# One core, an attention and FFN kernel: the engines' instruction lists searched anew past batch 0's k

## The chip, the cores and the metric

The kernel runs on one core of one Trainium2 chip. A core has TensorE (PE; its weight loads are shown as PEld), VectorE (DVE), ScalarE (ACT), GpSimd (POOL) and SyncE (SP), each with an instruction list of its own that it works through in order, and DMA queues. The metric is device time in microseconds (us); less is better.

## What is computed

Four batches of eight heads, 768 positions, 64 wide. A small 8 x 8 matrix per head is normalized five times over rows and columns, mixes the eight blocks of k and of v, and attention then stays inside each block of 96 positions. The result, 3072 tokens of 512, goes through a two-layer network.

```python
P = sort_net                                   # (4, 8, 8, 8), five times:
    P = exp(P - max); P = P / rowsum; P = P / colsum
k_sorted = einsum('bhij,bhjcd->bhicd', P, k_b) # the same for v
scores = (1 / 8) * q_b @ k_sorted^T            # inside each block of 96
attn = softmax(scores)
x = (attn @ v_sorted) as (3072, 512)
h = x @ w_in                                   # 512 -> 2048
g = max(h, 0) + alpha * min(h, 0)
out = g @ w_out                                # 2048 -> 512
```

## The kernel before

**The work.** There are 32 groups, one for each batch and block of 96 positions: groups 0 to 7 are batch 0. For each batch, k is prepared in six units: POOL spreads a unit into `KSz` (`conv_k`, L672), PE multiplies it by the mixing matrix (`prep_k`, a "k block", L685), ACT or DVE evicts it into `KT`. v is prepared in eight units: a copy into `VDz` (`conv_v`; for batch 0 into a part of `hT`, which is still free), a product on PE (`prep_v`, a "v block", L726), an eviction into `VS`. `VDz` has four slots and `KSz` three, so a copy waits until the product on its slot's old content is done. Batch 0 takes other forms of both (L656, L731).

**A group** (`attention`) takes scores on PE (s1, L772 for batch 0, L769 later), their maxima on DVE (`nm` or `nf`, L778), in batch 0 a second pass of scores with the maximum subtracted (s2, L793 and L784) and one exponential on ACT into `ET` (L816); in the later batches eight exponentials into `Esb` (L805), which a DMA transposition on SP's queue turns into `ET` (L810). Then PE multiplies by v (o, L825), DVE takes a reciprocal and scales (`rec`, `xq`, L833 and L836), and a transposition, on PE in batches 0 and 1 (tr, L851, copied into `xT`) and by DMA later (L844), gives the FFN's input. q of batches 1 to 3 is turned by six DMA transpositions each (`turn_q`, L465).

**The FFN.** FFN1 (`ffn1`, L875) takes chunks of groups: two chunks of two groups (192 columns), then seven of four (384 columns), each in 16 blocks of four matmuls into one of two PSUM banks of `psH` (the first chunk uses `psP` as a third); ACT takes the negative part (`t`, L885), DVE combines it into `hT` (L888). FFN2 (`ffn2`, L914) makes 24 tiles of 128 tokens, each in four parts of four matmuls, which are evicted to `outstg` and stored by SP. The last tile is made in two halves.

**The order.** Every operation is added to a graph with what it reads and writes. A table `SEQ` lists all 1226 operations by number, in one order from which each engine's list is read off; a letter behind a number gives the engine for those that may run on several (`p` POOL, `a` ACT, `d` DVE; none: the first that is allowed). `arrange` walks the table and computes a planned start for each. Semaphore waits follow from the graph. The table is data in the kernel: nothing is searched when it is built.

**Identity products.** `fill` and `idle` then look for gaps in the planned PE list and put matmuls with the identity there (`warm`, L1041), 512 columns each, into a PSUM bank that nobody reads. They compute nothing that is needed. In the trace there are 55 of them: 51 into `psYP`, three into `psH` and one into `psO`.

Of the kernel before, what the change touches and what calls it, by code (L numbers as in the profile page):

```python
# [7 lines left out]
AP = bass.AP  # L8
# [24 lines left out]
0 2 11 3 7 4 8 1 22 9 14 42 28 43 44 19 45 46 5 47 18 48 49 15 50 51 39 52 53 6 54 55 56 25 57 58 29 59 60 61  # L33
23 62 63 12 64 65 66 132 89 37 67 83 68 81 31 69 84 70 32 87 71 13 10 91 88 85 72 40 73 74 90 130 75 76 86 41
77 133 78 82 79 131 92 80 93 134 138 102 94d 103a 26 104 147 95 105a 100 148 98 96d 97 108 99a 38 101d 109d
158 159 118 106a 119d 107a 35 114 160 149 36 115d 116 16 120 117a 112a 146 150 111 110d 113d 161 30 17 122 27
135 123a 24 121a 128 144 124 129d 126 143 125a 151 127d 21 145 136 152 137 162 153 163 164 154 183 155 165
166a 34 156 184 20 157a 167 141 192 33 185 168 193 140 169 194 142 186 170 201 195 139 247 246 249 248 253 252
171 202 198 196 203 204 199 197 187 219 200 220 205 216 213 217 214 218 206 221 215 228 207 188 225 189 222
272 226 229 227 223 230 234 224 260 235 237 236 261 190 262 250 191a 238 269 208 309 270 231 251a 209 239 174  # L40
210 402 401 232 233 240 211 257 254 271 263 212d 255a 290 256 310d 278 264 258 291 273 346 259a 265 266 304
312d 292 279 267 280 303 241 268 293 284 242 281 243 301 282 337 347a 283 274 300 338 302a 244 299 287 245d
285 339 286 311 351d 294 340 313 295 305 296 275 314 288 315 289 319 276a 177 297 306d 316 320 321 307 317 378
298a 318 178 325 308a 379 322 341 323 348 342 182 380 326 324 354 349a 327 328 343 352 180 329 331 353d 381
344 350 345d 356 179 332 330 382 357a 334 383 333 372 335 181 359a 336 360 384 363 361 387 364 362 418 393 403
388a 385 365 366 419 369 358 367 373 370 368 420 374 386d 355d 428 371 394d 391 421 429 434 390d 444 431 392a
435 389 395 432 375 430 436 446 396d 452 445 376d 397 433 404 449 453 437 398a 454 464 447 458 465 399 459 455
474 176 400a 460 405 448 175 456 173 450 466 406 478 451d 422 457 475 476 482 172 423 467 504 424 461 483 494
484 505 462 425 407 477a 463 414 495 426a 480 485 572 573 408a 481d 438 409 486 548 412 439 496 487 508 506
277 440 491 479 417 534 410 411 509 413 416 535 415 507d 441 488 492 497 442d 524 493 489 510 490 515 511a 377  # L50
525 512 516 549 517 513 526 514 468 536 518 537d 521 469 470 519 527 560 520 538 471 561 539a 542 522 472d 571
543 523 498 540 562 550 499 570 500 541d 501 545 544 502a 563 574 546 554 575d 596 547 555 605 557 556 606a
611 503 578 558 576 551 559 579 427 612 580 581 552a 597 584 577 582 533 590 583 585 598 586 528 443 587 529
530 609 613 636 531 599 614 625 532d 608 591 610a 626 588 569 607 592 589 627 637 564 615 616 473 565 634 566
619 635a 628 567 617 638 568d 593 639a 618 620 640 622 641a 621 645 600 594a 676 643 601 658 623 595 677 642
661 659 624 644 678 662 602 663 660 670 679 703 671 603 704 664 604a 647 667 705 665d 648 629 666 691 630 631
692 713 672 668 706 669 712 738 685 739 715 673 686 693 714 687 674 740 675 632 716 633d 688 717 718 697 719d
752 689 741 767 698 690 680 751 749 699 700 553 649 750d 720 701 646 694 702 721 777 722 723 695a 768 753 696
726 780 754a 681 732 682 724 748 727 725 683 733 769 747 728 734 707 729 708 770 709 755 730 742 731 756 778
710 802 779a 812 757 758 782 776 759 761 760 781 735 762 783a 763 657 764 803 736a 813 651 784 814d 849 787  # L60
785 743 765 786 788 653 804 744 654 789 766 745 852 771 793 772 773 805 846 815 794 837 796 816a 795 811 774
790 797 656 798 817 799 853 818a 791d 819 800 838 650 825 820 847 801 839 826 821 655 822 848 806 850 840 807
831 808 652 851a 872 832 883 827 792 823 833 880 824 854 881a 886 834 855 828 856 835 836 884 860 910 885a
829d 857 861 873 882 711 866 858 862 874 887 867 859 911 908 863 909d 888 875 864 841 865 889 900 912 684 890
891 913a 842 901 894 892 746 868 893 902 869 843 844 876 870d 914 897 895 877 896 919 903 898 915d 916 878 934
917 920 879 935 980 918 936 809 981 899 928 775 925 929 904 830 930 926 921 927 960 737 931 961 922 932 937
905 962 906 942 933 982 907 945 923a 963 986 946 948 987 943 949 944 988 938 950 939 940 954 947 989 1006 955
957 1007 810 983 958 1008 959 951 956 971 952d 964 968 972 1009 984a 973 1017 969 965 845 1032 970 977 966 974
941 978 990 979 975 1018 985 976 997 1033 994 924 998 1019 999 995 967 996 1003 991 1000 1004 1020 1005 1001
1034 1002 1023 992 1014 993 1010 1046 1011 1015 1012 1024 1047 1035 1016 1058 1025 1026 871 1059 1029 1027  # L70
1013 1048 1028 1030 1060 1031 1040 1021d 1043 1078 1041 1061 1036 1044 1079 1037 1042 1022 1084 1045 1052 1085
953 1049 1053 1086 1054 1080 1038 1055 1050d 1066 1056 1087 1062 1067 1115 1063 1068 1104 1057 1072 1064 1069
1105 1065 1116 1070 1071 1106 1117 1075 1088 1118 1076 1107 1089 1073 1077 1081 1074 1039 1095 1090 1082a 1092
1096 1051 1136 1097 1093 1119a 1094 1101 1091 1108 1102 1098 1120 1103 1137 1099 1109 1100 1121 1083 1110 1112
1122 1111 1160 1123 1113 1114 1127 1124 1128 1138 1129 1125 1126 1133 1130 1134 1161 1135 1131 1132 1145 1142
1146 1162 1147 1143 1144 1139 1148 1163 1149 1140a 1150 1151 1141 1154 1152 1181 1153 1155 1156 1157 1166 1158
1202 1159 1167 1168 1182 1172 1169 1173 1208 1174 1170 1171 1178 1175 1179 1183 1180 1176 1177 1190 1187 1191
1184 1192 1188 1189 1196 1185a 1193 1186 1197 1209 1198 1194 1195 1210 1164d 1199 1165 1203 1200 1201 1204
1220 1211 1205 1212d 1221 1213 1206d 1222 1223 1207 1214 1224 1215 1216 1225 1217 1218 1219
# [41 lines left out]
class _Graph:  # L121
# [79 lines left out]
    def arrange(self, table):  # L201
        assert len(table) == len(self.ops)
# [5 lines left out]
        done = set()  # L208
        for x in table:
            op = self.ops[int(x.rstrip("pad"))]  # L210
            e = letters.get(x[-1], op.engs[0])
            assert e in op.engs and op.deps <= done
            done.add(op.idx)
            at = max(free[e], self.ready_at(op, e))
            op.eng, op.start, op.pos = e, at, len(self.order[e])
            free[e], op.end = self.span(op, e, at, free, loads)
            self.order[e].append(op)
        return max(op.end for op in self.ops)

    def fill(self, make, unit, first, spans):  # L220

        out, last = [], self.ops[first].end + 300
        for op in self.order["pe"]:
            for lo, hi in spans:
                begin = max(last, lo)
                n = int((op.start - begin) * 0.9 / unit)
                if op.start <= hi and n > 0:
                    x = _Op("pe", lambda e, n=n: make(e, n), n * unit, 0.0, None, len(self.ops))
                    x.start, x.end, x.banks = begin, begin + n * unit, set()
                    x.deps.add(first)  # L230
                    self.ops.append(x)
                    out.append(x)
            out.append(op)
            last = max(last, op.end)
        for pos, op in enumerate(out):
            op.pos = pos
        self.order["pe"] = out

    def idle(self, make, unit, banks, lo, hi, least):

        used = {k: sorted((op for op in self.ops if k in op.banks), key=lambda o: o.start) for k in banks}
        out, last = [], 0.0
        for op in self.order["pe"]:
            n = int((op.start - last) * 0.85 / unit)
# [841 lines left out]
```

## Time and profile before

| | |
|---|---|
| median of 3 runs | 241.96 us (241.48 to 242.43) |
| the profiled execution: own time, span | 242.12 us, 240.1 us |
| granted TensorE clock | 1.00 |
| PE busy by the page | 231.3 us |
| DVE, ACT, POOL busy by the page | 172.4, 153.9, 99.8 us |
| identity products into `psYP`, busy | 15.1 us (51) |
| HBM read, written | 27.28 MB, 6.29 MB |

The span is what the profile shows from the first instruction to the last; the execution's own time has about 2.0 us more around it. Matmuls are pipelined, so their busy times overlap, and start to start is what a block costs PE. In the chain of waits each piece lasts until the next begins. In a timeline row the columns are start, length, engine, line, operation, tiles, shapes and count, and in brackets the idle time before it with what ended that. L12 is line 12 of the kernel.

### The profile page before, as it was taken

The numbers are of one execution on the slowest core, as the hardware profiler recorded it, in microseconds if no ns is written. First come the engines' busy times: TensorE is split into PE (matmuls) and PEld (weight loads), VectorE is DVE, ScalarE is ACT, GpSimd is POOL, SyncE is SP. The second block draws the span as 40 slices with busy tenths as digits, with TensorE's granted clock in tenths as the row PEclk, the third lists the DMA queues.
The fourth block names the chain that finished last, engine by engine and source line by source line (L and its number), as shares of the span: only waits on it lengthen the run. The fifth ranks groups of instructions, "written<-read, shape, count | busy, mean of one in ns | idle before, by whom it ended". The sixth has DMA issues, their size and how long they took to land.

```text
span 240.1 us, 6229 instructions
## 1 busy us (share of the span) xinstructions
PE 231.3 (96%) x2519; PEld 142.3 (59%) x2519; DVE 172.4 (72%) x348; ACT 153.9 (64%) x422; POOL 99.8 (42%) x146
## 2 busy tenths in 40 slices
PE   7889998999999999999999999999999999999995
PEld 3446676688566656655666566555655555555554
DVE  4756887998989888777958677756777666645542
ACT  4576466678978788977667778567756655444510
POOL 7989707924689964518859841000000000000000
PEclk9999999999999999999999999999999999999999
DMA  5999999999967999999749974593745426101023
GB/s 101 205 211 217 155 220 197 176 180 166 161 118 141 144 128 163 161 180 164 153 101 69 114 137 79 111 183 64 141 121 112 123 49 177 39 0 44 0 91 131
DMA packets 71981, 31.36 MB, mean 131 GB/s; under 512 B 64512, under 2 KB 67344, under 8 KB 71952
## 3 DMA queue, kind: packets, MB, share of 16 engines
q0 software_dynamic: 23408, 13.63, 42.6%
q1 hardware_dynamic: 48544, 17.33, 35.2%
q8 instruction: 20, 0.33, 0.6%
q14 instruction: 9, 0.07, 0.1%
HBM read 27.28 MB, written 6.29 MB: 140 GB/s over the span
## 4 chain that ended last, share of the span: by engine, by line
PE 71%; POOL 11%; DMA 10%; DVE 5%; issue 1%; ACT 0%; POOLq 0%
PE psH L875 29%; PE psYP L914 27%; DMA KS<-in_k_dram 10%; POOL VDz L428 5%; PE psS L914 4%; PE psO L825 3%; PE psS L769 3%; PE psYP L726 2%; PE psYP L685 2%; DVE hT L888 1%; POOL KSz L672 1%; POOL w_in_bf L959 1%; POOL VDz L512 1%; DVE VDz L428 1%; PE psO L914 1%
## 5 line engine op out<-in xcount | busy, mean ns | idle before, releaser
L875 PE MATMUL psH<-xT,w_in_bf 128*128 128x384 bf16 (+1 forms) x556 | 98.4, 311 | 0.6 <-DVE hT L888 0.4
L888 DVE SCALAR_TENSOR_TENSOR hT<-t,omaT,psH 128x384 bf16<-128x384 f32 (+1 forms) x139 | 77.7, 571 | 29.2 <-ACT t L885 27.5
L885 ACT ACTIVATE t<-psH 128x384 f32<-128x384 f32 (+1 forms) x139 | 62.7, 461 | 50.5 <-PE psH L875 49.2
L914 PE MATMUL psYP<-w_out_bf,hT 128*128 128x512 bf16 x336 | 82.9, 379 | 0.0
L875 PEld LDWEIGHTS psH<-xT,w_in_bf 128*128 128x128 bf16 x556 | 49.0, 98 | 29.2 <-DVE hT L888 4.1
L914 PEld LDWEIGHTS psYP<-w_out_bf,hT 128*128 128x128 bf16 x336 | 31.1, 98 | 30.3 <-DVE outstg L428 0.6
L805 ACT ACTIVATE Esb<-psS,nf 96x96 bf16<-96x96 f32 x192 | 46.2, 344 | 2.0 <-DVE nf L778 1.8
L428 POOL COPY VDz<-VST 64x384 bf16<-64x384 bf16 x40 | 34.1, 853 | 15.6 <-PE psYP L726 12.8
L672 POOL COPY KSz<-KS 64x512 bf16<-64x512 bf16 x36 | 22.0, 612 | 18.8 <-PE psYP L685 8.8
L778 DVE TENSOR_REDUCE nf<-psS 96x8 f32<-96x768 f32 x24 | 22.8, 948 | 5.5 <-PE psS L769 5.1
L836 DVE TENSOR_TENSOR xq<-psO,rec 96x512 bf16<-96x512 f32 x31 | 21.2, 683 | 0.6
L457 POOL DMA_DIRECT2D QN<-in_q_dram x24 | 19.9, 837 | 0.3 <-POOL QN L517 0.3
L1041 PE MATMUL psYP<-identb 128*128 128x512 bf16 x51 | 15.1, 417 | 0.7 <-ACT identb L428 0.7
L825 PEld LDWEIGHTS psO<-VS,ET 112*128 112x128 bf16 x248 | 11.3, 98 | 4.7 <-DVE xT L428 0.7
L769 PEld LDWEIGHTS psS<-KT,QTz 128*96 128x96 bf16 x192 | 11.9, 125 | 2.5
L833 DVE RECIPROCAL rec<-psO 96x8 f32<-96x8 f32 x31 | 6.2, 200 | 9.8 <-PE psO L825 9.8
L825 PE MATMUL psO<-VS,ET 112*128 112x65 bf16 x248 | 12.7, 194 | 0.4 <-DVE xT L428 0.3
L769 PE MATMUL psS<-KT,QTz 128*96 128x96 bf16 x192 | 12.6, 209 | 0.0
L428 ACT ACTIVATE VS<-psYP 112x512 bf16<-112x512 f32 x15 | 10.3, 686 | 3.1 <-PE psYP L726 2.6
L428 ACT ACTIVATE KT<-psYP 128x512 bf16<-128x512 f32 x15 | 8.9, 596 | 3.8 <-PE psYP L685 2.5
L726 PEld LDWEIGHTS psYP<-BDV,VDz 128*128 128x128 bf16 x192 | 8.0, 98 | 3.6 <-POOL VDz L428 0.8
L726 PE MATMUL psYP<-BDV,VDz 128*128 128x64 bf16 x192 | 9.6, 193 | 0.5 <-POOL VDz L428 0.5
(142 smaller groups left out, 204.0 us busy)
## 6 DMA issues: line engine op xcount, KB each, us to landing
out_dram<-outstg SPq DMA_DIRECT2D x23, 256.0 KB, 2.6
KS<-in_k_dram POOLq DMA_DIRECT2D x3, 768.0 KB, 8.7
QN<-in_q_dram POOLq DMA_DIRECT2D x24, 96.0 KB, 3.8
w_in_bf<-in_moe_w_in_dram POOLq DMA_DIRECT2D x4, 512.0 KB, 11.9
w_out_bf<-in_moe_w_out_dram POOLq DMA_DIRECT2D x2, 1024.0 KB, 23.3
VST<-in_v_dram POOLq DMA_DIRECT2D x4, 384.0 KB, 18.3
hT<-in_q_dram POOLq DMA_DIRECT2D x1, 768.0 KB, 7.0
VST<-in_v_dram POOLq DMA_DIRECT2D x1, 768.0 KB, 10.9
```

Source lines behind the costliest of these rows:

```text
L428: return e.activation(o, i, ACTF.Copy) if e is nc.scalar else e.tensor_copy(o, i)
L672: G.add(POOL, lambda e, hp=hp: e.tensor_copy(AP(KSz, hp * 64 * 3072 + u % 3 * 1024 + hp * 64, [[3072, 64], [128, 8], [1, 64]]), AP(KS[n], ...
L726: inst = e.matmul(AP(t, off + dd * 64, [[row, 128], [1, 64]]), AP(VDz, (u % VSL * 8 + dd) * 128, [[VSL * 1024, 128], [1, 128]]), AP(BDV, b ...
L769: inst = e.matmul(o, AP(QTz[n], hp * 3072 + h4 * 768 + i * 96, [[6144, 128], [1, 96]]), AP(KT[n], (h4 * 8 + i) * bk, [[ld, 128], [64, 2], ...
L778: G.add(DVE, lambda e: e.tensor_reduce(AP(nx, 0, [[8, 96], [4, 2], [1, 4]]), AP(psX, 0, [[1024, 96], [512, 2], [96, 4], [1, 96]]), AxisLis ...
L805: inst = e.activation(AP(Esb[me], p * 128, [[1024, 96], [64, 2], [1, 48]]), AP(psX, (p // 4) * 512 + (p % 4) * 96, [[1024, 96], [48, 2], [ ...
L825: inst = e.matmul(AP(psZ, hp * 512 + h4 * 68, [[1024, 128], [1, 65]]), AP(ET[me] if far else ET[m], pos(h4, hp) * 96, [[800, nk], [1, 128] ...
L836: G.add(DVE, lambda e: e.tensor_tensor(out=AP(xq[me], 0, [[512, 96], [256, 2], [64, 4], [1, 64]]), in0=AP(psZ, 0, [[1024, 96], [512, 2], [ ...
L875: inst = e.matmul(AP(pt, poff, [[1024, 128], [1, n]]), AP(w_in_bf, kt * DFF + ft * 128, [[KT_TILES * DFF, 128], [1, 128]]), AP(xT, kt * XR ...
L885: G.add(ACT, lambda e: e.activation(AP(t1[tb], 0, [[384, 128], [1, n]]), AP(pt, poff, [[1024, 128], [1, n]]), ACTF.Relu, scale=-1.0), t_ac ...
L888: G.add(DVE, lambda e: e.scalar_tensor_tensor(out=AP(hT, ft * RING + tok % RING, [[FT_TILES * RING, 128], [1, n]]), in0=AP(t1[tb], 0, [[38 ...
L914: inst = e.matmul(AP(bank[0], bank[1], [[1024, 128], [1, n]]), AP(hT, ft * RING + tok % RING, [[FT_TILES * RING, 128], [1, 128]]), AP(w_ou ...
```

## The change

The table `SEQ` is another from the place on where batch 0's k has been prepared, for all five engines. Ahead of that place (about 16 us in the trace) the lists are the same, except that what `fill` put there now stands in the table as entries. An entry such as `i3G` is three identity products into the bank with the letter G; `filler` makes an operation of it that waits for those who read that bank, and `fill` and `idle` are gone. The new table has 49 identity products: 31 up to and just behind batch 0's last k block, as before, and 18 more, the last two ahead of s2 of group 2.

Three kinds of operation may now run on more engines: batch 0's q evictions on ACT or DVE, batch 0's eight v copies and the copy `KTpad` on POOL, ACT or DVE. In the table, `KTpad` goes from POOL to DVE; of batch 0's v copies ACT has units 5, 0, 3, 4 and 6 (before 0, 1 and 6), DVE 1 and 2 (before 3, 4 and 7) and POOL 7 (before 2 and 5). The q evictions stay on ACT. The DMA transpositions were taken as longer in the search that gave the table; no duration in the kernel's code is changed for that.

Part of PE's list, from o of group 0 to the first v block of batch 1 (`1.3` is block 3 of FFN1's chunk 1; `t0.1` part 1 of FFN2's tile 0; `k2` k block 2 of batch 1; `I` identity products):

```
before: o0 s1(2) tr1 tr0 spread 1.0 s2(2) 1.3 1.1 1.2 s1(3) o2 1.6 1.5 1.4 s2(3) 1.9 1.8 1.7 t0.0 1.11 1.12 s1(4)
  tr2 k0 1.15 o3 1.10 s2(4) tr3 k1 1.13 s1(5) 2.0 k2 t0.1 1.14 s2(5) o4 2.2 2.1 k3 s1(6) t0.2 tr4 2.3 s2(6) o5 2.4
  k4 t0.3 2.6 tr5 2.5 k5 s1(7) 2.8 2.7 o6 v0
after:  o0 tr1 s1(2) I spread tr0 I s2(2) 1.0 1.1 1.2 s1(3) 1.3 o2 s2(3) 1.6 1.5 1.4 s1(4) tr2 1.9 1.8 o3 1.7 s2(4)
  1.11 tr3 1.10 1.12 s1(5) o4 k0 t0.0 1.15 k1 1.13 s2(5) k2 tr4 2.0 t0.1 s1(6) 1.14 2.2 2.1 o5 s2(6) 2.4 k3 2.3
  t0.2 tr5 k4 2.5 2.6 o6 s1(7) k5 2.7 2.8 t0.3 v0
```

POOL's list has batch 2's v copies in one row ahead of its eight q loads and its k copies; before, q loads and two k copies stood between them. On SP's queue, the store of FFN2's tile 1 and three of batch 1's six q turns move among the transpositions of groups 8 to 10; before, all six turns stood ahead of them. At the end PE has tile 23's second half and tiles 22 and 21 ahead of tile 20's last two parts, then tile 23's first half; before it was tiles 20, 22, 21, and both halves of tile 23.

```diff
 SEQ = """
-0 2 11 3 7 4 8 1 22 9 14 42 28 43 44 19 45 46 5 47 18 48 49 15 50 51 39 52 53 6 54 55 56 25 57 58 29 59 60 61
...
+0 2 11 7 3 4 1 8 9 i15Y 22 42 28 14 43 44 45 46 19 47 18 48 5 49 50 51 15 39 52 53 54 6 55 56 57 25 58 29 59
...
+    def filler(self, x, used, make, unit, first):
+        n, bank = int(x[1:-1]), x[-1]
+        written, free = used.get(bank, (False, []))
+        assert not written or free
+        op = _Op(("pe",), lambda e: make(e, n, bank), n * unit, 0.0, None, len(self.ops))
+        op.banks, op.deps = set(), {first, *free}
+        self.ops.append(op)
+        return op
...
-        loads = [0.0, 0.0, {"n": 2, "mark": 193, "usable": 0.0, "end": 0.0, "fills": True}]
+        loads = [0.0, 0.0, {"n": 2, "mark": 193, "usable": 0.0, "end": 0.0, "fills": False}]
...
         for x in table:
-            op = self.ops[int(x.rstrip("pad"))]
-            e = letters.get(x[-1], op.engs[0])
+            if x[0] == "i":
+                op = self.filler(x, used, make, unit, first)
+                e = "pe"
+            else:
+                op = self.ops[int(x.rstrip("pad"))]
+                e = letters.get(x[-1], op.engs[0])
             assert e in op.engs and op.deps <= done
             done.add(op.idx)
+            for k in op.banks:
+                k = names.get(k, k)
+                used[k] = (True, [] if e == "pe" else used[k][1] + [op.idx])
...
-    def fill(self, make, unit, first, spans):
...
-    def idle(self, make, unit, banks, lo, hi, least):
...
+    ANY = ("pool", "act", "dve")
...
-        G.add(ACT, lambda e: copy(e, o, i), t_act(512), r=keys, w=[("Q0", u)], prio=prio)
+        G.add(EITHER, lambda e: copy(e, o, i), t_either(512), r=keys, w=[("Q0", u)], prio=prio)
...
-            G.add(POOL, lambda e: e.tensor_copy(AP(KT[0], 48, [[ld, 128], [bk, 32], [1, 16]]),
-                                                AP(KT[0], 0, [[ld, 128], [bk, 32], [1, 16]])), 900,
+            G.add(ANY, lambda e: copy(e, AP(KT[0], 48, [[ld, 128], [bk, 32], [1, 16]]),
+                                      AP(KT[0], 0, [[ld, 128], [bk, 32], [1, 16]])), {"pool": 610, "act": 613, "dve": 430},
...
-            G.add(POOL if u % 3 == 2 else EITHER, lambda e: copy(e, o, i), {"act": 858, "dve": 540, "pool": 860},
+            G.add(ANY, lambda e: copy(e, o, i), {"act": 858, "dve": 540, "pool": 860},
...
-    G.fill(warm, 215, ident_op, [(5000, first_y[0].start), (ffn_ops[0].start + 1, ffn_ops[1].start)])
-    G.idle(warm, 215, {"psY": (psYP, 0), ("psP", 0): (psYP, 512), ("psH", 0): (psH, 0), ("psH", 1): (psH, 512),
-                       "psO0": (psO, 0), "psO1": (psO, 512)}, first_y[0].start, 84e3, 300)
+    total = G.arrange(SEQ, {k: x[0] for k, x in banks.items()}, warm, 215, ident_op)
```

More of the change, by code (lines that the diff above doesn't have):

```diff
@@ L38 @@
[L38 to L42, printed above, removed]
@@ L80 @@
+1147 1142 1138 1143 1144 1151 1148 1152 1139 1153 1149 1150 1157 1140d 1220 1158 1154 1141 1159 1181 1155 1156
[3 rows of a table added]
 """.split()
@@ L218, in arrange @@
         return max(op.end for op in self.ops)
-    def fill(self, make, unit, first, spans):
[L222 to L237, printed above, removed]
-    def idle(self, make, unit, banks, lo, hi, least):
[L241 to L244, printed above, removed]
-            if lo <= last and op.start <= hi and op.start - last >= least and n > 0:
-                for k, bank in banks.items():
-                    before = [u for u in used[k] if u.start < last]
-                    after = [u for u in used[k] if u.start >= last]
-                    free = [u for u in before if u.eng != "pe" and u.end + 46 > last]
-                    if not before or before[-1].eng == "pe" or free or not after or after[0].eng != "pe":
-                        continue
-                    x = _Op("pe", lambda e, n=n, bank=bank: make(e, n, bank), n * unit, 0.0, None, len(self.ops))
-                    x.start, x.end, x.banks = last, last + n * unit, {k}
-                    while before and before[-1].eng != "pe":
-                        x.deps.add(before.pop().idx)
-                    self.ops.append(x)
-                    out.append(x)
-                    break
-            out.append(op)
-            last = max(last, op.end)
-        for pos, op in enumerate(out):
-            op.pos = pos
-        self.order["pe"] = out
     def emit(self, nc, sems):
```

89 lines of the change are left out of this document (42 added, 47 removed), and 13 rows, old and new, of the table SEQ.

## The prediction

> **What bounds the kernel now.** I read the page first, then the chain of waits, then TensorE's timeline from 16 us on, and beside it those of ACT, DVE and POOL.
>
> ```profile
> PE 231.3 (96%) x2519; PEld 142.3 (59%) x2519; DVE 172.4 (72%) x348; ACT 153.9 (64%) x422; POOL 99.8 (42%) x146
> PEclk9999999999999999999999999999999999999999
> ```
>
> TensorE (PE) is at work nearly throughout, at its full granted clock. A busy PE is not one that does something needed, though: identity products count as busy, and a matmul's shown length (0.4 us and more) overlaps its follower's. So I take the pace of each kind of block from the chain of waits, where a piece lasts until the next begins (start, us, what):
>
> ```profile
> 51.07 0.17 PE psO L851 x4
> 51.25 0.33 PE psH L875 x4
> 51.58 0.23 PE psYP L685 x8
> 51.81 0.31 PE psS L772 x8
> ...
> 52.96 0.24 PE psO L825 x8
> ...
> 53.43 0.34 PE psS L793 x8
> 53.77 0.54 PE psS L784 x8
> ...
> 56.75 0.86 PE psYP L914 x4
> ```
>
> These are a 192-column block of the first FFN product (0.33), a transposition on PE (0.17), a k block (0.23; I take a v block alike), scores s1 (0.31), attn·v (o, 0.24), scores s2 (0.34 and 0.54; the latter holds 0.09 of the next wait, so I count 0.79 for the pair) and a quarter of an FFN2 tile (0.86).
>
> Next come places where the old and the new PE list have exactly the same blocks behind them, since only there can two orders be compared by the clock. Counting the entries of both lists I find: o of group 0 (25.93), o of group 2 (31.49), the first v block of batch 1 (53.03), block 13 of FFN1's second chunk (57.45 + 0.33 = 57.78), the first v block of batch 2 (69.22) and block 10 of the third chunk (78.70 + 0.65 = 79.35). PE's timeline there, and at its waits and identity products (L1041):
>
> ```profile
> 22.02 1.25 PE L1041 MATMUL psYP<-identb 128*128 128x512 bf16 x5
> ...
> 25.93 0.42 PE L825 MATMUL psO<-VS,ET 112*128 112x65 bf16 x8
> ...
> 28.66 0.50 PE L875 MATMUL psH<-xT,w_in_bf 128*128 128x192 bf16 x4
> ...
> 31.49 0.42 PE L825 MATMUL psO<-VS,ET 112*128 112x65 bf16 x8
> ...
> 38.23 0.40 PE L685 MATMUL psYP<-BDM,KSz 128*128 128x64 bf16 x8 [0.92 <-POOL KSz L672]
> ...
> 49.05 0.59 PE L1041 MATMUL psYP<-identb 128*128 128x512 bf16 x2
> ...
> 53.03 0.40 PE L726 MATMUL psYP<-BDV,VDz 128*128 128x64 bf16 x8
> ...
> 55.21 0.38 PE L1041 MATMUL psYP<-identb 128*128 128x512 bf16 x1
> 55.66 0.41 PE L726 MATMUL psYP<-BDV,VDz 128*128 128x64 bf16 x8
> ...
> 57.45 0.82 PE L875 MATMUL psH<-xT,w_in_bf 128*128 128x192 bf16 x8
> ...
> 69.22 0.40 PE L726 MATMUL psYP<-BDV,VDz 128*128 128x64 bf16 x8
> ...
> 77.61 0.38 PE L1041 MATMUL psYP<-identb 128*128 128x512 bf16 x1
> 78.46 0.41 PE L726 MATMUL psYP<-BDV,VDz 128*128 128x64 bf16 x8 [0.47 <-POOL VDz L428]
> 78.70 1.46 PE L875 MATMUL psH<-xT,w_in_bf 128*128 128x384 bf16 x8
> ...
> 84.78 0.42 PE L825 MATMUL psO<-VS,ET 112*128 112x65 bf16 x8 [0.31 <-DVE xT L428]
> ```
>
> From about 57 us on nearly everything on PE touches its neighbour. No order can shorten PE's own blocks, which are the same in both kernels, so what is to be won is the waits and identity products, and most lie ahead of 57 us.
>
> **Stretch 1, to o of group 2.** Batch 0's v must be copied out (8 copies), multiplied (8 PE blocks) and evicted (8 VS copies) before o of groups 1 and 0.
>
> ```profile
> 16.73 1.62 ACT L428 ACTIVATE hT<-VST 128x384 bf16<-128x384 bf16 x2 [0.19 <-DMA VST<-in_v_dram]
> ...
> 22.30 1.24 ACT L428 ACTIVATE VS<-psO 112x512 bf16<-112x512 f32 x2
> ...
> 25.07 0.81 ACT L816 ACTIVATE ET<-psS 112x768 bf16<-112x768 f32 x1 [0.44 <-PE psS L784]
> ```
>
> The new lists give ACT five of the eight copies (u = 5, 0, 3, 4, 6; before: 0, 1, 6) at 0.81 each. Its list is: two copies, two VS evictions (0.62 each), copy 3, VS 1, copies 4 and 6, ET of group 1, VS 4. From 16.73 that is 5 × 0.81 + 3 × 0.62 + 0.81 + 0.62 = 7.3, and with 0.5 of waiting for the first two PE blocks ACT leaves VS 4 at 24.5. The v block of u = 7 writes the bank that VS 4 reads, and that of u = 6 stands behind it on PE: 25.15. VS 6 on ACT ends at about 26.0, o of group 1 runs at 26.05, three identity products follow (five took 1.25 with the last one's overlap, so 0.65), and o of group 0 comes at 26.95. Before it came at 25.93, so this part is 1.0 late. The stretch after it is shorter: the same blocks, with 3 identity products, take 4.8 by my count (the s2 of group 2 waits for its maximum until 29.2, four FFN1 blocks and s1 of group 3 follow) against 31.49 − 25.93 = 5.56. So o of group 2 stands at 31.8 against 31.49: **0.3 lost**. KTpad, moved from POOL to DVE, and the two identity products put ahead of s1 of group 1 make that s1 late by up to 0.5; ACT's list covers it, and without that cover it would be lost.
>
> **Stretch 2, to the first v block of batch 1.** Both lists hold 21 FFN1 blocks, 4 FFN2 quarters, 6 k blocks, 4 s1, 4 s2, 5 o and 4 transpositions here: 6.9 + 3.4 + 1.4 + 1.2 + 3.2 + 1.2 + 0.7 = 18.0 us. Before took 53.03 − 31.49 = 21.5, so 3.5 went to waits and identity products, 0.92 of it at 38.23.
>
> ```profile
> 36.81 3.96 POOL L672 COPY KSz<-KS 64x512 bf16<-64x512 bf16 x6 [8.37 <-DMA KS<-in_k_dram]
> ```
>
> Batch 1's k lands at 36.8 in both, since the loads ahead of it are issued in the same order. Before has 12 FFN1 blocks, an FFN2 quarter and little attention to do until then and runs dry; the new list puts s2 of group 4, s1 of group 5, o of groups 3 and 4, a transposition and one more FFN1 block ahead of the first k block and the FFN2 quarter behind it, and gets there at 39.1, when KSz has been ready for a microsecond. Walking the new list block by block with ACT's and DVE's lists beside it, I count waits of PE in seven places: for the maxima of groups 3, 4 and 6 (0.4, 0.3 and 0.3; DVE gets s1 of group 3 at 31.5 and has its maximum 0.9 later, when PE has been free since 32.0) and for the banks of FFN1 blocks 3, 9, 10 and 14 (0.2 each, until DVE has read them). That is 1.8, of which 0.1 overlaps, so 19.7 for the stretch. The first v block then stands at 51.5: **1.5 won** by there.
>
> Part of it comes from DVE (the stage's row: us, busy PE, PEld, DVE, ACT, POOL):
>
> ```profile
> 40.00:50.00 10.00, 9.59 (x152) 7.29 (x151) 9.54 (x20) 6.78 (x15) 8.05 (x13) 1.00 1.77 187
> ```
> ```profile
> 41.11 0.97 DVE L428 COPY VDz<-VST 64x384 bf16<-64x384 bf16 x1
> ...
> 61.69 0.54 DVE L428 COPY VDz<-VST 64x384 bf16<-64x384 bf16 x1
> ```
>
> The same copy took DVE 0.97 beside POOL's copies and 0.54 without them, and DVE had 9.54 of 10 us filled there. Four of DVE's six such copies go to ACT (about 3.5 us off DVE by the 0.97 and its like), and seven PSUM evictions of some 0.6 come from ACT, one of tile 1 goes back: DVE's load stays level, but the slow copies no longer stand ahead of FFN1's evictions. In the Trainium skill, "GPSIMD Engine Reference", Key points, GpSimd shares its SBUF interfaces with VectorE, with contention for DVE instructions in a two-port mode or with two SBUF inputs. By that rule KTpad, now on DVE beside POOL, would be slowed like the VDz copy; the sum stays, as ACT sets the end of stretch 1, and the 0.97 against 0.54 agrees with the rule.
>
> **Stretch 3, to 79 us.** To block 13 the new list needs 4.2 (work 4.1) against 4.75, mostly the 0.45 at 55.21: 2.1 won. To the first v block of batch 2 the work is 11.0 and before took 11.4: 2.2. To block 10 the work is 9.2 and before took 10.1, with 0.85 at 77.61 where PE stood before POOL's VDz:
>
> ```profile
> 62.39 11.36 POOL L428 COPY VDz<-VST 64x384 bf16<-64x384 bf16 x12 [1.57 <-PE psYP L726]
> ...
> 84.08 0.87 POOL L428 COPY VDz<-VST 64x384 bf16<-64x384 bf16 x1
> ```
>
> Before, POOL mixes the q loads and two KSz copies with the last VDz copies, and the last ends at 85. The new list does all sixteen VDz copies first; at 0.9 each with the waits for free slots they end at 76.5, ahead of every v block by 1 us or more, and the eight q loads behind them end at 83, no later than before. So the 0.85 goes: **3.0 won** by block 10.
>
> **Stretch 4, to the end.**
>
> ```profile
> 60.00:90.00 30.00, 29.14 (x325) 18.05 (x324) 26.55 (x50) 24.61 (x77) 25.15 (x32) 1.00 0.99 139
> 90.00:140.00 50.00, 49.80 (x483) 30.42 (x482) 37.15 (x66) 37.62 (x111) 32.05 (x46) 1.00 1.01 140
> ```
>
> PE is idle for 0.86 here to 90 us, 0.47 of it at 78.46, and for 0.20 to 140, so 0.6 is left after 79 us; waits that hide in a matmul's overlap may make it 1.2. The new order could win that or lose as much elsewhere. I have not walked it block by block and take nothing.
>
> **The tail.** Before, tile 20 is long stored and tile 23's other half evicted when PE makes the last half; now tile 20 is finished just ahead of that half.
>
> ```profile
> 235.45 1.91 PE L914 MATMUL psS<-w_out_bf,hT 128*128 128x256 bf16 x16
> ...
> 237.40 0.38 ACT L428 ACTIVATE outstg<-psS 128x256 f32<-128x256 f32 x1 [6.46 <-PE psS L914]
> ```
>
> Its eviction is hidden by the 1.91 of those 16 products, but its 256 KB store overlaps the last 128 KB one: 0 to 0.3 lost, I take 0.2.
>
> **The sum.** 3.0 − 0.2 = 2.8. My walk has no lateness of its own, and the trace shows pieces of 0.1 that it leaves out; I take 2.4. The profiled execution had 242.12 (span 240.1 and 2.0 around it), 0.16 above the median of 241.96; against the median I forecast 239.6.
>
> **Rivals.** *The waits move, they don't go* (chance 0.17). DVE's load stays level around 40 to 50 us and ACT's grows; if FFN1's banks wait for them as before, or if ACT's five v copies cost stretch 1 another microsecond, stretches 1 and 2 give nothing and only POOL's 0.85 and bits of stretch 3 remain: 241.0 to 242.2, no measurable change. Against it: more attention work stands ahead of the first k block, whatever the evictions do.
>
> *Transpositions come late, on the slower side* (0.1). SP issues its queue in order. The new one has tile 1's store ahead of the first ET transposition (group 8), and turns of q between the next ones.
>
> ```profile
> 60.11 1.93 ACT L805 ACTIVATE Esb<-psS,nf 96x96 bf16<-96x96 f32 x8
> ```
> ```profile
> ET<-Esb SPq DMA_TRANSPOSE x24, 3.0
> ```
>
> By my walk ACT has Esb of group 8 done at 62.2, then tile 1's copy at 62.8; the store goes, the transposition is issued at 63.2 and lands 3.0 later, at 66.2; PE reaches o of group 8 at 68.8. The slack is 2.6. If landing took 6.1 instead of 3.0, PE would stand 0.5 there, and so at each of the eight groups of batch 1, which pass through the same queue: 4.0 lost against 2.4 won, 243.6. It decides from a landing of 5.6 on. For it speaks the in-order queue, against it the median of 24.
>
> *The clock falls* (0.03, within no change). There are 49 identity products instead of 55. If PE ran at half pace for four FFN2 quarters, that would cost 4 × 0.86 = 3.4: 243.0. The rows show full clock in every slice, with waits up to 0.92 us, and I count none over 1 us. In the Trainium skill, "TensorE: Matmul & The Clock Gate", Part 1, it takes an idle window of about 3.4 us to halve the clock; no run here shows such a window.
>
> *The last stage wins too* (0.13, inside faster): 3.0 + 1.2 = 4.2 with no loss in the tail, 237.8.
>
> **How the numbers follow.** A measurement of this kernel tells about 0.5% (1.2 us) from no change, so faster means under 240.75 and slower over 243.2. The forecast has 0.57, the late gain 0.13: faster 0.7. Waits that move and the clock make same 0.2, late transpositions slower 0.1. The range reaches from the late gain, 237.8, over the case without change to 242.3.
>
> **What would show it.** In the new profile: o of group 0 about 27, o of group 2 near 31.8, the first k block near 39 without a wait for KSz, the first v blocks of batches 1 and 2 near 51.5 and 67, no wait for VDz near 75, no L1041 after 30 us. I am wrong if the first v block of batch 1 stands at 53 or later, or if new waits for ET, QTz or KSz on PE show after 80 us.

## The result, and the profile after

| | before | after |
|---|---|---|
| median of 5 runs each, same chip | 241.97 us (241.48 to 242.43) | 238.09 us (237.76 to 238.75) |
| profiled execution: own time, span | 242.12, 240.1 us | 238.10, 236.4 us |

The ratio is 0.9842, 95% interval 0.9822 to 0.9861: 3.9 us won, where 2.4 was forecast (239.6, range 237.8 to 242.3). Runs that were slowed as a whole are left out of the ratios below (seven of twelve in x2_new_from_76).

The page of the kernel after shows the busy time by engine, the clock by slices, and the chain of waits by engine. Below it stands, from the page before, the same line of the chain.

```profile
PE 227.3 (96%) x2483; PEld 141.6 (60%) x2513; DVE 167.4 (71%) x343; ACT 158.7 (67%) x429; POOL 99.0 (42%) x144
PEclk9999999999999999999999999999999999999999
PE 85%; DMA 5%; ACT 4%; DVE 2%; POOL 2%; issue 2%; POOLq 0%
```
```profile
PE 71%; POOL 11%; DMA 10%; DVE 5%; issue 1%; ACT 0%; POOLq 0%
```

The chain that ends last was 21% POOL and DMA and is now 7%. PE's timeline of the kernel after, at the places where the prediction compared both lists (some FFN2 matmuls have no record here, so the busy sums of PE are not compared):

```profile
26.48 0.42 PE L797 MATMUL psO<-VS,ET 112*128 112x65 bf16 x8
...
31.94 0.41 PE L797 MATMUL psO<-VS,ET 112*128 112x65 bf16 x8
...
39.40 0.40 PE L657 MATMUL psYP<-BDM,KSz 128*128 128x64 bf16 x8
...
51.94 0.40 PE L698 MATMUL psYP<-BDV,VDz 128*128 128x64 bf16 x8
...
67.43 0.40 PE L698 MATMUL psYP<-BDV,VDz 128*128 128x64 bf16 x8
...
76.01 1.47 PE L847 MATMUL psH<-xT,w_in_bf 128*128 128x384 bf16 x8
...
135.28 1.14 PE L847 MATMUL psH<-xT,w_in_bf 128*128 128x384 bf16 x6 [0.46 <-DVE rec L805]
...
231.75 1.91 PE L886 MATMUL psS<-w_out_bf,hT 128*128 128x256 bf16 x16
```

These are o of groups 0 and 2, the first k block of batch 1 (no wait for KSz now), the first v blocks of batches 1 and 2, blocks 11 and 10 of FFN1's third chunk (block 10 at 76.01 + 0.65 = 76.66), a wait in a later chunk, and the last 16 products. Against the rows of before (us; "ahead" is how much earlier the kernel after gets there):

| place | before | after | ahead | forecast |
|---|---|---|---|---|
| o of group 2 | 31.49 | 31.94 | -0.45 | -0.3 |
| first v block, batch 1 | 53.03 | 51.94 | 1.09 | 1.5 |
| first v block, batch 2 | 69.22 | 67.43 | 1.79 | 2.2 |
| block 10, third chunk | 79.36 | 76.66 | 2.70 | 3.0 |
| last 16 products | 235.45 | 231.75 | 3.70 | 3.0 |
| span | 240.1 | 236.4 | 3.7 | 2.8 (less 0.4 for what the walk left out) |

Up to block 10 the walk holds within 0.4. Behind it a microsecond was won that the sum had at nothing. The span gives 3.7 of the 3.9; the rest lies outside it (2.0 around the span before, 1.7 after), and no run here shows what made it.

POOL's timeline after shows the new row: the last eleven of batch 2's sixteen v copies in one go, then eight q loads, then k.

```profile
67.89 9.99 POOL L400 COPY VDz<-VST 64x384 bf16<-64x384 bf16 x11 [1.29 <-PE psYP L698]
77.83 6.58 POOL L429 DMA_DIRECT2D QN<-in_q_dram  x8
84.33 5.45 POOL L644 COPY KSz<-KS 64x512 bf16<-64x512 bf16 x8
```

The last copy ends at 77.9 (forecast 76.5) and the q loads at 84.4 (forecast 83); no PE row near 75 waits for VDz.

### The profile page after: what moved, and what is told of

The parts are those of the page before. It is cut to its first block, busy times and chain, and to the rows that moved or that the text cites. A ratio compares the mean times of both kernels' runs of the same rounds, so it can differ in the third digit from the quotient of the medians.

```text
span 236.4 us, 6202 instructions
## 1 busy us (share of the span) xinstructions
PE 227.3 (96%) x2483; PEld 141.6 (60%) x2513; DVE 167.4 (71%) x343; ACT 158.7 (67%) x429; POOL 99.0 (42%) x144
## 4 chain that ended last, share of the span: by engine, by line
PE 85%; DMA 5%; ACT 4%; DVE 2%; POOL 2%; issue 2%; POOLq 0%
PE psH L847 34%; PE psYP L886 30%; DMA VST<-in_v_dram 5%; PE psS L886 4%; PE psS L741 4%; PE psO L797 3%; PE psYP L698 2%; PE psYP L657 2%; ACT hT L400 2%; PE psS L756 2%; PE psS L765 1%; PE psO L823 1%; ACT VS L400 1%; POOL VDz L484 1%; DVE nm L750 1%
## 5 line engine op out<-in xcount | busy, mean ns | idle before, releaser
L886 PE MATMUL psYP<-w_out_bf,hT 128*128 128x512 bf16 x308 | 78.6, 379 | 1.6 <-issue 0.2
L400 ACT ACTIVATE outstg<-psYP 128x512 f32<-128x512 f32 x18 | 10.8, 598 | 5.3 <-PE psYP L886 5.1
L1017 PE MATMUL psYP<-identb 128*128 128x512 bf16 x46 | 13.3, 420 | 0.7 <-ACT identb L400 0.7
L400 DVE CAST VS<-psYP 112x512 bf16<-112x512 f32 x15 | 10.3, 689 | 3.0 <-PE psYP L703 2.1
```

Source lines behind the costliest of these rows:

```text
L400: return e.activation(o, i, ACTF.Copy) if e is nc.scalar else e.tensor_copy(o, i)
L886: inst = e.matmul(AP(bank[0], bank[1], [[1024, 128], [1, n]]), AP(hT, ft * RING + tok % RING, [[FT_TILES * RING, 128], [1, 128]]), AP(w_ou ...
```

## Experiments

All are built on the code of the kernel after with other lists, so engines and banks can be set at will. A "seam" is the place where the list of one kernel is joined to that of the other. Ratios are against runs of the kernel before in the same session (medians 242.0 to 242.2). Positions of the profiled executions (us; the first v copy on ACT shows when batch 0's v has landed):

| kernel | first v copy | o, group 2 | first k, b1 | first v, b1 | first v, b2 | block 10 | span |
|---|---|---|---|---|---|---|---|
| before | 16.73 | 31.49 | 38.23 | 53.03 | 69.22 | 79.36 | 240.1 |
| after | 16.50 | 31.94 | 39.40 | 51.94 | 67.43 | 76.66 | 236.4 |
| e1_new_head | 16.93 | 32.47 | 39.67 | 52.06 | 68.68 | 78.79 | 239.4 |
| e2_old_head | 16.21 | 31.08 | 37.96 | 53.07 | 68.99 | 78.22 | 238.1 |
| c1_old_to_o2 | 17.35 | 32.39 | 40.18 | 53.00 | 68.49 | 77.72 | 237.3 |
| x4_k0_later | 17.07 | 32.28 | 39.30 | 53.03 | 69.22 | 79.36 | 240.1 |
| e9_copies_dve | 16.34 | 31.73 | 38.93 | 51.99 | 69.35 | 78.59 | 238.5 |
| e7_no_late_identity | 16.35 | 34.36 | 41.91 | 54.28 | 69.79 | 79.02 | 239.2 |

### Does each stretch keep what it wins? Lists joined at a place

```
e1_new_head:   all five lists of after up to batch 1's first v block, then those of before
e2_old_head:   those of before up to there, then those of after
e3_new_to_76:  those of after up to block 11 of the third chunk, then those of before
x2_new_from_76: those of before up to there, then those of after
```

> All engines' lists of the kernel after up to the first v block of batch 1 (51.9 us there, 53.0 before), then those of the kernel before. Theory that the gains belong to their stretches and add: 1.1 was won by that place, so 242.0 - 1.1 = 240.9, and PE's first v block stands at 51.9. Rival, that the old POOL list further on sets the time near 77 us whatever comes before: the microsecond is given back there as a longer wait for VDz (0.47 before, then 1.5), 242.0.

241.48 us, ratio 0.9977 (0.9957 to 0.9997). The head comes 0.97 early (52.06 against 53.03); behind the seam the timeline of PE has

```profile
52.73 0.61 PE L756 MATMUL psS<-identb,nm 96*112 96x96 bf16 x8
53.59 0.50 PE L847 MATMUL psH<-xT,w_in_bf 128*128 128x192 bf16 x4 [0.25 <-DVE hT L860]
```

because the old list asks there for a bank that DVE, in the new head's order, has not read. From there the lead is 0.51 to 0.61 at every place (block 10: 79.36 - 78.79 = 0.57), to the end. So nothing near 77 us takes it back, and nothing adds to it: the rival falls, and the sum by stretches holds but for what the seam costs.

> The reverse: lists of the kernel before up to the first v block of batch 1, then those of the kernel after. If the gains add, 238.1 + 1.1 = 239.2, with the first v block at 53.0. Rival, that the new lists fit only what the new head leaves behind (v and k of batch 1 prepared in another order, other engines ahead or behind): 240 to 241.

239.54 us, ratio 0.9883 (0.985 to 0.9915), close to the 239.2 of the sum: on an old head the later lists are worth 2.5 by the medians. In the profiled execution it is 2.0 of span, where 3.7 - 1.1 = 2.6 were expected; 0.57 of that is lost by the second v block, which comes 2.51 behind the first here and 1.94 in the kernel after.

> Lists of the kernel after up to block 11 of the third FFN1 chunk (76.0 us there, 78.7 before), then those of the kernel before. My sum had no gain behind this place; the traces show 1.0 more, most of it from 79 to 100 us. If that gain belongs to the order there, this kernel gives 242.0 - 2.7 = 239.3. Rival, that it only follows from being ahead (POOL's v copies of batch 2 done, so that q and k of batch 2 are early): 238.3.

242.97 us, ratio 1.0034 (1.0012 to 1.0055). 2.3 ahead at block 10, it lost 3.8 by 93 us: POOL, its v copies done in the new order, made k of u = 1, two more v copies and the remaining q loads before k of u = 0, and the old PE list stood for 2.26 before that. PE's timeline and the windows (us, busy PE, PEld, DVE, ACT, POOL, PE clock, DMA share, GB/s):

```profile
87.29 0.41 PE L657 MATMUL psYP<-BDM,KSz 128*128 128x64 bf16 x8 [2.26 <-POOL KSz L644]
```
```profile
84.52:87.93 3.41, 1.15 (x15) 0.61 (x13) 0.77 (x3) 1.03 (x3) 2.61 (x4) 1.00 2.02 165
87.93:91.34 3.41, 3.41 (x25) 2.21 (x24) 1.64 (x3) 1.41 (x3) 1.45 (x3) 0.50 0.79 67
```

The granted clock fell to 0.50 some 0.65 us after PE had gone on, for 3.4 us (87.9 to 91.3), and made the rest of the loss. Three of the twelve runs kept a mean clock of 0.999 or more and took 241.40 to 242.69; the nine others, at 0.992 or 0.993, took 242.89 to 243.91. So even with the clock up this kernel misses the expected 239.3. It tells nothing of the late gain; it tells what a seam costs.

> Lists of the kernel before up to block 11 of the third FFN1 chunk (78.7 us), then those of the kernel after. If what the traces show behind that place (1.0 to 1.1, which my sum had at nothing) belongs to the order there, the time is 242.0 - 1.0 = 241.0. Rival, that it only comes with the lead won before: 242.0. At the seam two orders meet (in the first seam kernel that cost 0.5, in the third an idle PE of 2.3 us), so milestones behind it count more than the total.

Its twelve runs spread from 240.56 to 248.28 (ratio of five of them 0.9974, 0.9946 to 1.0002), so the total decides nothing. In the profile, PE's weight loads were 0.09 ahead of before at 71 us, 0.83 near 86 and 1.25 near 99: 1.16 won behind the seam with no lead to start from. So the late gain belongs to the order there. Then PE stood for 2.47 up to 114.86, because batch 3's v, loaded by POOL 0.5 later than in the kernel after, landed some 6 us later (last section); why is not settled.

```
c1_old_to_o2:  lists of before up to o of group 2, then those of after
```

> Lists of the kernel before up to o of group 2 (31.5 us; 31.9 in the kernel after), then those of the kernel after: batch 0's v copies and KTpad are on their old engines again. The new head loses 0.45 by that place, so if it has no use later this beats both kernels: 238.1 - 0.4 = 237.7. Rival, that the later list needs what the new head leaves ready (maxima of groups 2 and 3, FFN1's first blocks), or that the wait for batch 1's k near 38 us takes it back: 238.1 to 238.6.

238.8 us, ratio 0.9876 (0.9844 to 0.9908): not better than the kernel after. Two of the six runs had a mean clock of 0.992 and 0.993 (240.19, 239.93); the four others took 237.69 to 239.03, which is no gain either. In the profiled execution batch 0's v landed late, so that o of group 2 came at 32.39, as late as e1's 32.47 with the new head; yet the first v block stood at 53.00, and at 52.06 in e1. From o of group 2 to that block it took 20.61 here, 20.00 in the kernel after and 19.59 in e1: in these traces the 0.45 that the new head costs buys 0.6 to 1.0 behind it. Here s2 of group 3 waits 0.70 for its maximum, and 0.37 in the kernel after; the rest is spread. The first expectation falls.

### The VDz wait at 77.6 and its neighbours

```diff
 e4_pool_new (lists of before; POOL):
-v copies of batch 2, among them 8 q loads and k of u = 1
+v copies of batch 2 in after's order, 8 q loads, k from u = 0 on
 e5_pool_old (lists of after; POOL): the reverse
 x1_dve_swap (lists of before; DVE):
-nf(13) xT(10)
+xT(10) nf(13)
 x3_row_and_swap (lists of before): x1's exchange, and on POOL
+v copies of batch 2 in before's order, 8 q loads, k of u = 0, 1, then as before
```

> The kernel before with only one stretch of POOL's list changed: batch 2's v copies in one row ahead of the eight q loads and the k copies, as in the kernel after. By my prediction's step that takes the 0.85 us at 77.6 (an identity product and a wait for VDz) and nothing else: 241.1. Rival one, that the later gain of 1.0 is POOL's too (VDz is also what the last v blocks near 81 to 85 wait for): 240.1. Rival two, that PE takes the time back at the next wait (for xT at 84.8, where DVE is late): 241.7 or more.

242.21 us, ratio 1.0004 (0.9988 to 1.002): no change. The 0.85 went, but the timeline of PE has a new wait ahead of it, since after's row makes u = 1 later than before's PE list wants it:

```profile
71.14 0.41 PE L699 MATMUL psYP<-BDV,VDz 128*128 128x64 bf16 x8 [0.73 <-POOL VDz L401]
```

> The kernel before with two neighbours in DVE's list exchanged: group 10's xT copy now ahead of group 13's maximum. Before, PE ended an FFN1 block at 84.29 and began o of group 11 at 84.78, since that needs the PSUM bank that the xT copy reads, and the copy stood behind the maximum's 0.95. Theory, that the late gain of the new lists is made of such single places: the 0.49 goes and the time is 241.5. Rival, that the maximum, now 0.34 later, makes Esb and the next banks late by as much: 242.0.

242.24 us, ratio 1.0009 (0.9994 to 1.0024): no change. o of group 11 comes 0.61 earlier (84.17 against 84.78), but the v block behind it only 0.14 (84.89 against 85.03):

```profile
84.17 0.41 PE L798 MATMUL psO<-VS,ET 112*128 112x65 bf16 x8
84.89 0.41 PE L699 MATMUL psYP<-BDV,VDz 128*128 128x64 bf16 x8 [0.30 <-POOL VDz L401]
```

The wait for xT had hidden one for POOL's last v copy.

> The kernel before with two edits at once: POOL makes batch 2's v copies in one row, in their old order of u (so that u = 1 is not late), the q loads and then k's u = 0 and 1 behind it; and the exchange on DVE of group 10's xT copy and group 13's maximum. Each was tried alone with no gain: POOL's row in the new order won its 0.85 at 77.6 and lost 0.95 at 71.1 before VDz; the exchange won 0.58 at 84.8 and lost 0.63 on the next product, which waits for the last VDz copy on POOL. Theory, that single waits hide one another, so that only both together pay: 0.85 + 0.49 go, 240.7, no wait for VDz from 69 to 88. Rival, that a third wait (k's KSz or FFN1's banks near 88) takes it back: 241.5 to 242.0.

241.69 us, ratio 0.9977 (0.9961 to 0.9994). Both waits for VDz are gone, PE is 1.28 further ahead at 83.8 us than it was at 71, and then

```profile
85.92 0.34 PE L824 MATMUL psO<-identb,xq 96*128 96x96 bf16 x4 [0.49 <-DVE xq L809]
```

takes 0.57 back: 0.6 kept in the profile, 0.5 in the runs. So each of three waits hid the next, as in the theory, and the rival's third wait is there too, on DVE's xq; the time is in the rival's range. The old order loses its time near 84 us to a stack of waits from two engines, and neither of the two single edits paid.

> The kernel after with POOL's old order of batch 2's v copies, q loads and k copies put back (the reverse of the run with POOL's new order in the old lists, which gave 242.2: its 0.85 at 77.6 went, and a wait of 0.73 for VDz came at 71.1, because the copies of u = 1 stand later in the new row). If POOL's order and PE's order are a pair, PE now stands before VDz or KSz: 0.85 and more is lost, 239.0 to 241. Rival, that POOL has slack here, now that PE's order is another: 238.1.

244.03 us, ratio 1.009 (1.0055 to 1.0125). The pair shows from the other side: PE's new order with POOL's old one stands for 3.29.

```profile
78.64 0.61 PE L698 MATMUL psYP<-BDV,VDz 128*128 128x64 bf16 x8 [3.29 <-POOL VDz L400]
```
```profile
75.00:78.60 3.60, 0.35 (x3) 0.00 (x0) 1.51 (x3) 0.74 (x2) 3.44 (x6) 0.94 1.15 107
78.60:81.60 3.00, 2.96 (x26) 2.15 (x27) 0.95 (x1) 1.22 (x3) 2.96 (x4) 0.51 0.57 39
```

The clock fell again, for 3.4 us from 78.1 on. In all 5.4 of span is lost against the kernel after. The wait makes most of it: the one run of six with a mean clock of 1.00 took 242.76, against 238.09 for the kernel after.

### What stretch 2 rests on

```diff
 x4_k0_later (lists of before; PE):
-k0 1.15 o3 1.10 s2(4)
+1.15 o3 1.10 k0 s2(4)
 e9_copies_dve (table of after, four entries):
-310 351 355 390
+310d 351d 355d 390d
```

> The kernel before with one entry of PE's list moved: batch 1's first k block goes behind FFN1 block 15, o of group 3 and FFN1 block 10, which stood behind it. Before, PE was idle for 0.92 ahead of that block (38.23) while KSz was copied; those three take 0.9. Theory, that stretch 2's gain is mainly this order of ready work ahead of a late landing: some 0.65 won at 39.4, and carried to the end, 241.3. Rival, that the FFN1 and attention work so moved is missing later, or that POOL's three KSz slots or DVE make the wait up before 53: 242.0.

242.26 us, ratio 1.0005 (0.9985 to 1.0025): no change. The wait for KSz is gone, but the first v block stands at 53.03, the very place of before. Its head was 0.8 late, which an unchanged list makes up at the KSz wait (x1_dve_swap, 0.26 late at o of group 2, had its first v block at 52.83). In the other kernels with before's lists up to there, that block stood between 52.67 and 53.27. So what is won at 38.23 is not kept: something else sets the time up to 53.

> The kernel after with four of batch 1's VDz copies (u = 0, 3, 4, 6, second halves) back from ACT on DVE, at the same places of the order. By my prediction's reason for stretch 2 they stand ahead of FFN1's evictions on a DVE that has no room (9.7 of 10 us busy from 40 to 50 in the kernel after), at 0.5 to 0.97 each: 2 to 3.5 us more for DVE, of which PE loses some 1.0 before the first v blocks are through: 239.1. Rival, that stretch 2's gain is the order of attention against k alone and DVE has slack at those places: 238.1 to 238.3.

240.4 us, ratio 0.9927 (0.99 to 0.9955) against 0.9842: 2.1 lost, twice what was expected. The windows of this kernel, then of the kernel after:

```profile
50.00:60.00 10.00, 8.69 (x123) 6.50 (x125) 9.53 (x24) 4.98 (x14) 2.44 (x3) 1.00 0.71 125
```
```profile
50.00:60.00 10.00, 9.74 (x146) 7.62 (x148) 9.02 (x23) 8.68 (x18) 3.58 (x5) 1.00 0.73 128
```

and PE's timeline of e9_copies_dve:

```profile
52.68 0.50 PE L847 MATMUL psH<-xT,w_in_bf 128*128 128x192 bf16 x4 [0.29 <-DVE hT L860]
...
55.01 0.41 PE L698 MATMUL psYP<-BDV,VDz 128*128 128x64 bf16 x8 [0.45 <-DVE VS L400]
...
59.99 0.26 PE L847 MATMUL psH<-xT,w_in_bf 128*128 128x192 bf16 x1 [0.43 <-DVE hT L860]
```

FFN1's banks and v's bank wait for DVE, while ACT has half its time free. The place differs from what I wrote: 0.2 of head start is used up by the first v block (51.99), and 1.9 goes behind it, by batch 2's first v block (69.35 against 67.43), while v of batch 1 is prepared. The engine that makes those copies is worth more than any single move in the order that was tried here.

### The identity products

```diff
 e7_no_late_identity (table of after): the eight entries past batch 0's last k block out, 18 products
-i2Y i2Y i3Y i2Y i3Y i3G i1P i2Y
```

> The kernel after without its last 18 identity products (all from batch 0's first s1 on to s2 of group 2); everything else as it was. If they only fill waits: 238.1, with idle PE of up to 1.3 us in their places. Clock rival: two runs of this study had the clock at 0.50 for 3.4 us after PE had stood for 2.3 and 3.3 us in one piece; if the many shorter waits between 17 and 29 us do the same, 3.4 us at half pace cost 1.7: 239.8, more if it happens twice. A gain (237.8) if the last product of a group delays a needed block.

240.47 us, ratio 0.9943 (0.9921 to 0.9964) against 0.9842: 2.4 lost. Windows without them, then of the kernel after:

```profile
16.00:22.40 6.40, 4.38 (x128) 3.28 (x128) 4.72 (x9) 5.86 (x11) 6.05 (x8) 0.97 1.07 214
22.40:28.00 5.60, 4.01 (x79) 3.47 (x76) 2.47 (x7) 2.95 (x6) 3.71 (x6) 0.50 1.05 171
28.00:36.00 8.00, 7.90 (x89) 6.51 (x88) 6.26 (x16) 2.79 (x7) 0.00 (x0) 0.52 1.14 217
```
```profile
16.00:22.40 6.40, 6.00 (x135) 3.60 (x134) 3.87 (x9) 5.62 (x9) 5.73 (x7) 1.00 1.06 213
22.40:28.00 5.60, 5.09 (x102) 3.18 (x96) 3.40 (x9) 3.60 (x7) 4.46 (x7) 1.00 1.07 170
28.00:36.00 8.00, 7.41 (x115) 5.91 (x115) 7.30 (x20) 4.25 (x11) 0.00 (x0) 1.00 1.13 215
```

From about 22.0 to 35.7, by the shares of the first and last window, the clock was 0.50: 13.7 us, four times the 3.4 of e3 and e5. All twelve runs had it down for part (means 0.957 to 0.979); the five runs of the kernel after had 0.999 or 1.000. PE's timeline has these two as the longest idle pieces, one ahead of the fall and one behind it:

```profile
21.33 0.23 PE L940 MATMUL psYP<-identf,alphaR 16*128 16x16 f32 x1 [0.79 <-DVE VS L400]
...
23.84 1.06 PE L703 MATMUL psO<-BDK,hT 128*64 128x64 bf16 x32 [1.12 <-ACT VS L400]
```

Up to the fall nothing is late: the v products behind the first of these rows start at 21.81, against 21.96 in the kernel after. "They only fill waits" falls; the clock rival is right, at more than its price. o of group 2 comes 2.4 later, and that is kept (2.36 at block 10).

## Why the prediction was right, and where its size was off

**Sign and mechanism** were right: waits ahead of 80 us went, no VDz wait was left near 75, and no identity product stands past 30 us. No row of PE past 80 us waits for ET, QTz or KSz, which would have shown the prediction wrong. The forecast of 239.6 missed 1.5 us of a gain of 3.9.

**The step that failed is stretch 4**, "I have not walked it block by block and take nothing". From block 10 to the last 16 products the lead grew from 2.70 to 3.70 (by PE's weight loads it was 3.8 near 100 us and 4.1 near 120, before some was given back), and x2_new_from_76 found 1.16 there without any lead to start from. The bounds in that part (0.6 visible, 1.2 with hidden waits) held the value; I chose the end at zero. The rival "the last stage wins too" (237.8) comes nearest. Where the gain lies can be counted: summing the blocks of both lists at the prediction's paces (an estimate, good to about 0.2), the kernel after is 2.5 to 2.9 ahead from block 10 to 83.5 us of before, and 3.45 at 84.78; x2_new_from_76 is -0.1 to 0.3 ahead and then 0.87. So about half of it is the wait for xT there, which neither of them has. The prediction quoted that row with 0.31, by the matmuls; the row of before's weight loads has

```profile
84.78 0.30 PEld L825 LDWEIGHTS psO<-VS,ET 112*128 112x128 bf16 x8 [0.69 <-DVE xT L428]
```

What hid the gain is in x1 and x3: this was the visible one of three stacked waits. What was given back: FFN1's wait at 135.28 is shown against DVE's rec, but the code makes that block wait for the transposed xT and not for rec. The last of its DMAs was issued at 129.0 and took 6.2, as the answer on that tile for 124 to 137 us has it:

```profile
L816 SPq DMA_TRANSPOSE xT<-xq x2: 1570/1761/1952, 127.0 to 129.0; - x2
...
DMA to landing us min/median/max: 6.2/6.2/6.2
```

The median of all sixteen xT transpositions is 2.4. "Transpositions come late" was thus real at one place, worth 0.46, not 4.0: batch 1's ETs were issued from 63.8 (forecast 63.2), landed within 4.4 in the window from 60 to 75 us, and o of group 8 stood at 69.2 (forecast 68.8).

**Stretch 1** was right by luck, as two errors cancel: o of group 0 came at 26.48, not 26.95, and the part behind it took 5.46, not 4.8. That the head is 0.45 behind at o of group 2 is no loss by itself: c1_old_to_o2 undid it and won nothing.

**Stretch 2** took 51.94 - 31.94 = 20.0 against 19.7, and from the first v block of batch 1 to block 10 it was 24.72 against 24.8 (26.3 before, less the 1.5 that the sum took there; its counts of work alone, 4.2 + 11.0 + 9.2, would have given 24.4): the totals were good to 0.3. The waits behind the first of them were not all the ones counted. For the stretch, the weight loads of PE waited (us in total, times, longest; five rows of before, then the rows of after):

```profile
PEld psYP L685 <- DVE hT L888: 1.0, 1, 1.0
PEld psS L772 <- ACT ET L816: 0.4, 1, 0.4
PEld psYP L875 <- DVE hT L888: 0.4, 2, 0.2
PEld psH L875 <- DVE hT L888: 0.4, 1, 0.4
PEld psYP L875 <- ACT KT L428: 0.3, 1, 0.3
```
```profile
PEld psS L765 <- DVE nm L750: 1.1, 4, 0.5
PEld psS L744 <- ACT t L857: 0.6, 2, 0.4
PEld psS L744 <- ACT ET L788: 0.2, 1, 0.2
```

The wait of the first k block (1.0; PE's own row names KSz) and 1.1 at FFN1's banks are gone. The maxima cost 1.1, where 1.0 was counted; the 0.8 counted for FFN1's banks is not in the rows, and 0.8 ahead of scores s1, which was not counted, is. That the total came out so near is luck in part. Of the prediction's reasons, the DVE copies stood the test, at twice the expected worth, but with 0.3 of it in this stretch (20.26 in e9_copies_dve) and the rest behind; the attention ahead of the first k block, alone, did not (x4_k0_later). So no single edit shows what took the 1.5 out of this stretch. The 0.4 taken off for pieces left out was about what the walk missed by block 10, and the tail cost no visible time (0.2 taken).

**The rival on the clock** had a wrong condition, idle time in one piece of over 1 us; the new table keeps the clock since its 18 products are where they are.

**Not settled:** which moves shortened stretch 2, which hold the rest of the late gain from 85 to 100 us, and why batch 3's v landed late in x2_new_from_76. None of the variants beat the kernel after.

## What to carry to other kernels

Compare two orders at places where the same work is done on both sides, and walk every stretch, also the one that looks full: a visible wait of 0.3 can have two more behind it, and each of two single exchanges here only moved the time to the next wait. An order is one object: of seven kernels that joined parts of the two, none was faster than the whole new one, and two were slower than the old. Before taking filler matmuls out, look at the clock with them gone.

## What the runs showed of the hardware

- **Clock.** It fell to 0.50 after an idle piece of PE of 2.26 us (e3), in one of 3.29 (e5), and in e7 where the longest ahead of the fall was 0.79. It stayed at 1.00 through one of 2.47 in x2_new_from_76. So the length of one piece does not decide. Each fall lasted 3.4 us or four times that, and by the clock's records in the traces the times between its changes are whole multiples of 3.41 (24, 1 and 44 in e3, 69 in x2). Stretches of that length, laid end to end from the clock's first rise, hold the idle piece of e3 whole in one (84.52 to 87.93, PE busy for 1.15 of 3.41) and that of x2 in two, the emptier with 1.51 busy. The stretch ahead of e7's fall, then x2's, with x2's wait:

```profile
18.66:22.07 3.41, 2.21 (x75) 1.78 (x69) 1.99 (x3) 3.41 (x6) 3.41 (x6) 1.00 1.07 215
```
```profile
112.96:116.37 3.41, 1.51 (x15) 0.94 (x16) 0.61 (x1) 0.41 (x1) 3.07 (x4) 1.00 1.15 276
114.86 0.41 PE L698 MATMUL psYP<-BDV,VDz 128*128 128x64 bf16 x8 [2.47 <-POOL VDz L400]
```

  PE's busy time in a stretch does not decide alone either: e7 lost the clock with more of it than x2 kept it with. What does is not settled: e7's stretch holds mostly matmuls of 112 columns and fewer, x2's by time mostly those of the FFN, but no run varies that alone. In the Trainium skill, "TensorE: Matmul & The Clock Gate", Part 1, the clock is halved after an idle window of about 3.4 us. The length of the falls agrees with such a window; that PE must stand idle through one does not: here 1.15 and 2.21 us of work in it did not keep the clock. In e7 PE was busy for 7.90 of 8.00 us and the clock still at 0.52.
- **Landing times.** With nearly the same lists ahead, batch 0's first v copy began between 15.99 and 17.35 over the profiled executions. And the loads of batch 3's v (POOL's timeline of x2_new_from_76, then of the kernel after) were issued 0.5 later and the first copy of them came 6.2 later:

```profile
97.73 2.14 POOL L463 DMA_DIRECT2D VST<-in_v_dram  x4 [2.08 <-DMA QTz<-QN]
113.11 6.22 POOL L400 COPY VDz<-VST 64x384 bf16<-64x384 bf16 x7 [13.24 <-DMA VST<-in_v_dram]
```
```profile
97.20 2.14 POOL L463 DMA_DIRECT2D VST<-in_v_dram  x4 [4.14 <-DMA QTz<-QN]
106.94 6.29 POOL L400 COPY VDz<-VST 64x384 bf16<-64x384 bf16 x7 [7.59 <-DMA VST<-in_v_dram]
```
